# Value rows loaded once into three sets of slots, their block means made from the slots, and a byte copy that joins the first expert's weights

## The chip, the cores and the metric

The kernel runs on one core of a Trainium2 chip. The metric is the device time of one execution in microseconds (us): 640.8 us, the median of three runs (639.45 to 641.47).

## What is computed

Three stages follow each other. Sparse attention on two batches, 8 heads, 768 positions and 64 values a head: a query sees the keys less than 16 positions away and, for each of the 24 blocks of 32 positions, the maximum of the block's keys; the values are the local ones and the block means of v. Then a first expert with the Mish activation, then a second one with a product of two projections.

```
k_sum = k.reshape(B, H, nb, 32, D).max(axis=3)
v_sum = v.reshape(B, H, nb, 32, D).mean(axis=3)
mask_l = abs(pos[:, None] - pos[None, :]) < 16
scores_s = scale * einsum('bhsd,bhnd->bhsn', q, k_sum) + log(32)
a = softmax(concatenate([where(mask_l, scale * q k^T, -1e9), scores_s]))
x = a @ concatenate([v, v_sum])            # 1536 tokens x 512
h = x @ w_in; x = (h * tanh(softplus(h))) @ w_out     # d_ff 2048
out = ((x @ w_a) * (x @ w_b)) @ w_out2                # d_ff 1536
```

The weights of the experts arrive as 64-bit floats and every product of an expert is made of three matmuls of rounded 32-bit parts (high by high, low by high, high by low).

## The kernel before

**Attention** goes through six groups of 256 queries, three for each batch (g0 to g2, g3 to g5), and in each group through four pairs of heads, which gives 24 small batches, numbered here from 0. For each of them TensorE makes the scores (`batch_s`, lines 509 and 513, 16 matmuls), VectorE adds the mask (line 524), ScalarE takes four exponentials (line 531), VectorE divides (lines 534 to 538), TensorE transposes (`batch_o`, line 553, 4 instructions), ScalarE or VectorE copies the result out of PSUM, and TensorE multiplies by the values (line 566, 8 matmuls). A matmul of plain 32-bit floats is two instructions in the trace (x8 is four of them). The result is split into a rounded high part and a rest (lines 578 and 579), the input of the first expert.

**The values** lie in two sets of slots (`vw_o`), 120 partitions high: 96 window rows of v for each of four units of 64 queries, and 24 rows for the block means. `load_windows` loads the windows (576 to 768 KB a group, the first and last unit of a batch by a DMA of 160 KB of its own). The means come from a second reading of v: `prep_v` loads a batch of v in three pieces of 512 KB into borrowed slots and multiplies them by a pooling matrix (line 443, 24 matmuls a batch), `keep_v` copies the result from PSUM, and `spread_v` copies it into both sets of slots by four DMAs of 48 KB each on SyncE's queue, 8 in a batch.

**The first expert's weights** are cut into 16 slices of `w_in` and 16 of `w_out`. `load_w` loads a slice (512 KB) into one of three staging slots, joins the two 32-bit words of each number (ScalarE at line 604, VectorE at lines 606, 609 and 612), and writes the rounded high part (line 618) and the rest (line 620) into a slot of 1024 columns. Slices 0 to 4 are used by three blocks of tokens in turn (256, 256 and 512 tokens), between and beside the batches of attention.

**The order** is written by a planner, `Plan`: each operation has a key (a due time), costs and dependencies, and `emit` hands each engine its instructions in the order that the planner's model gives. On the chip every engine, and SyncE's queue of DMAs, goes through its list in that order and waits at the head. Until the planner's time 21 it puts in dummy matmuls (`fill`, line 397) where TensorE would be free.

The diff touches `Plan.emit` (line 206), the slots (lines 269, 310, 316), `dma`, `consts`, `prep_v`, `keep_v`, `spread_v`, `load_windows`, `batch_o`, `load_w` and the due times from line 687.

Of the kernel before, what the change touches and what calls it, by code (L numbers as in the profile page):

```python
# [14 lines left out]
I32 = mybir.dt.int32  # L15
AF = mybir.ActivationFunctionType
# [18 lines left out]
class Plan:  # L35
# [49 lines left out]
    def emit(self):  # L85
# [32 lines left out]
        while done < n:  # L118
# [84 lines left out]
            if delay:  # L203
                dma_free = max(dma_free, end + self.DMA_LEAD) + delay
                end = dma_free + self.DMA_TAIL
                landed.append(end)
# [18 lines left out]
def attention_mish_moe_bilinear_moe(  # L225
# [23 lines left out]
    U = 64  # L249
# [19 lines left out]
    TOT, N_BASE, N_EXT = 53184, 16, 10  # L269
# [40 lines left out]
    vw_o = [take(GU * HD) for _ in range(2)]  # L310
# [5 lines left out]
    NPO = 2 * NB - P // BLK  # L316
# [14 lines left out]
    def dma(key, dst, src, r=(), w=(), nbytes=0):  # L331
        pl.add(key, [("SP", 0.48, lambda env: nc.sync.dma_start(out=dst, in_=src))],  # L332
               r=r, w=w, delay=nbytes / 3.3e5)
# [24 lines left out]
    def consts(env):  # L358

        nc.gpsimd.memset(mask, 0.0)  # L360
        nc.gpsimd.memset(mask[:, :, WK:SW], math.log(BLK) / SCALE)
        for h in range(2):
            m = mask[h * U:(h + 1) * U, :, 0:WK]
            nc.gpsimd.affine_select(
                out=m, in_=m, pattern=[[0, 3], [1, WK]], base=-1,
                channel_multiplier=-1, compare_op=ALU.is_ge, fill=NEG)
            nc.gpsimd.affine_select(
                out=m, in_=m, pattern=[[0, 3], [-1, WK]], base=2 * WIN - 1,
                channel_multiplier=1, compare_op=ALU.is_ge, fill=NEG)
# [10 lines left out]
        mid = pool[:, C0:C0 + P // BLK]  # L380
        nc.gpsimd.memset(mid, 1.0 / BLK)
        nc.gpsimd.affine_select(out=mid, in_=mid, pattern=[[-BLK, P // BLK]], base=0,
                                channel_multiplier=1, compare_op=ALU.is_ge, fill=0.0)
        nc.gpsimd.affine_select(out=mid, in_=mid, pattern=[[BLK, P // BLK]], base=BLK - 1,
                                channel_multiplier=-1, compare_op=ALU.is_ge, fill=0.0)
# [43 lines left out]
    def prep_v(key, kd, b, pieces):  # L429


        name = ("vs", b)
        t0 = 0
        for o, n in pieces:
            src = v[b, t0 * P:(t0 + n) * P, :].rearrange("(t p) c -> p t c", p=P)
            dma(kd + 0.01 * t0, ar(o, n, HD), src, w=[sb(o, n * HD)], nbytes=n * P * HD * 4)
            for i in range(n):
                t = t0 + i

                def mm(env, t=t, o=o, i=i):  # L440
                    c = C0 - P // BLK * t
                    for p in range(NP):
                        nc.tensor.matmul(bank[env[name]][32 * p:32 * p + NB, 0:P], pool[:, c:c + NB],  # L443
                                         ar(o + i * HD + p * P, P), start=(t == 0), stop=(t == S // P - 1),
                                         skip_group_check=True)

                pe(key, 0.3, mm, r=[sb(pool_o, NPO), sb(o, n * HD)], w=[name],
                   alloc=(name,) if t == 0 else ())
            t0 += n
        assert t0 == S // P  # L450

    def keep_v(key, b):
        name = ("vs", b)
        copy(key, P, lambda env: ar(vm_o, P), lambda env: bank[env[name]][:, 0:P], w=[name, sb(vm_o, P)], free=[name])

    def spread_v(key, s):

        for p in range(NP):
            src = ar(vm_o, P)[32 * p:32 * p + NB, :].unsqueeze(1).to_broadcast([NB, GU, P])
            dma(key + 0.01 * p, ar(vw_o[s], GU, HD)[WK:SW, :, p * P:(p + 1) * P], src,  # L460
                r=[sb(vm_o, P)], w=[("vsum", s, p)], nbytes=NB * GU * P * 4)

    def load_windows(key, g):

        b, gi = divmod(g, NG)
        s = g % 2
# [76 lines left out]
    def batch_o(key, g, p):  # L543
# [15 lines left out]
        vs = g % 2  # L559
# [27 lines left out]
    def load_w(first, kind, c):  # L587
# [9 lines left out]
        if BITS64:  # L597
# [6 lines left out]
            act(key, 512, lambda env: nc.scalar.activation(out=hw, in_=hw, func=AF.Copy, scale=2.0 ** -112),  # L604
                r=[sb(so, 1024)], w=[("hw", so)])
            dve(key, 512, lambda env: nc.vector.tensor_scalar(
                out=f.bitcast(U32), in0=f.bitcast(U32), scalar1=29, scalar2=None,
                op0=ALU.logical_shift_right), fast=True, r=[sb(so, 1024)], w=[("f", so)])
            dve(key, 512, lambda env: nc.vector.scalar_tensor_tensor(  # L609
                out=f.bitcast(U32), in0=hw.bitcast(U32), scalar=3, in1=f.bitcast(U32),  # L610
                op0=ALU.logical_shift_left, op1=ALU.bitwise_or), r=[("hw", so), sb(so, 1024)], w=[("f", so)])
            dve(key, 512, lambda env: nc.vector.scalar_tensor_tensor(  # L612
                out=f.bitcast(U32), in0=hw.bitcast(U32), scalar=0x80000000, in1=f.bitcast(U32),
                op0=ALU.bitwise_and, op1=ALU.bitwise_or), r=[("hw", so), sb(so, 1024)], w=[("f", so)])
        else:
            f = ar(so, 512)
            dma(key - 3.0, f, w_dram[kind][c], w=[sb(so, 512), ("f", so)], nbytes=P * 2048)
        copy(key, 512, lambda env: r32(ar(o + 512, 512)), lambda env: f, fast=True, only='ACT',
             r=[("f", so), sb(so, 1024)] + ext, w=[sb(o + 512, 512)])
        dve(key, 512, lambda env: nc.vector.tensor_sub(out=r32(ar(o, 512)), in0=f, in1=ar(o + 512, 512)),  # L620
            r=[sb(o + 512, 512), ("f", so), sb(so, 1024)], w=[sb(o, 512)])
# [66 lines left out]
    for b in range(B):  # L688
        g0 = NG * b
        if b == 0:  # L690
            pieces = [(T_S[0], 2), (T_S[2], 2), (T_L[1], 2)]
            kv, kd, ev = 8.0, 6.0, 1.5
        else:
            pieces = [(T_S[0], 2), (Y1, 2), (T_S[0], 2)]
            kv, kd = bt[g0, 0] - 8.0, bt[g0, 0] - 16.0
            ev = end_o(g0 - 2)
        at_time(ev, lambda kv=kv, kd=kd, b=b, x=pieces: prep_v(kv, kd, b, x))
        at_time(ev, lambda kv=kv, b=b: keep_v(kv + 0.5, b))
        for i in range(2):
            ev = end_o(g0 - 2 + i) if b else 1.6  # L700
            at_time(ev, lambda k=max(kv, ev), x=(g0 + i) % 2: spread_v(k + 1.0, x))
# [5 lines left out]
    for g in range(B * NG):  # L707
        kq, kw = (0.6, 4.0) if g == 0 else (bt[g, 0] - 10.0, bt[g, 0] - 4.0)
        at_time(end_s(g - 2) if g >= 2 else 1.0, lambda k=kq, g=g: load_q(k, g))
        at_time(end_o(g - 2) if g >= 2 else 1.5, lambda k=kw, g=g: load_windows(k, g))  # L710
# [246 lines left out]
```

## Time and profile before

| | us |
|---|---|
| median of three runs | 640.8 |
| the profiled execution | 640.17 |
| its span, first to last instruction | 638.1 |
| TensorE busy | 624.9 |
| VectorE busy | 319.1 |
| ScalarE busy | 264.0 |
| GpSimd busy | 6.5 |

The span is 2.07 us shorter than the execution's own time. TensorE is busy for 98% of it; the page's slices show the other engines and the DMA engines busy in the first quarter and mostly free later. Matmuls of dummies count as busy too, so the first slices are to be read by line.

### The profile page before, as it was taken

What the parts mean: (1) busy time and instruction counts of PE and PEld (TensorE: products, weight loads), DVE (VectorE), ACT (ScalarE), POOL (GpSimd) and SP (SyncE); (2) the same over time, 40 slices, a digit from 0 to 9 for tenths busy, and PEclk for the clock granted to TensorE, in tenths of its full rate; (3) what the DMA queues carried; (4) which work ended last, traced back from release to release, by engine and by line L of the source; (5) the groups of instructions that cost most, each with busy time, mean ns of one, the idle gap of its engine ahead of it and who ended that gap; (6) DMA issues with size and microseconds to landing.
All of it is one profiled execution on the core that took longest, in us unless ns stands there. A gap on an engine that the chain in (4) does not pass through costs nothing.

```text
span 638.1 us, 9894 instructions
## 1 busy us (share of the span) xinstructions
PE 624.9 (98%) x3966; PEld 514.1 (81%) x3969; DVE 319.1 (50%) x749; ACT 264.0 (41%) x577; POOL 6.5 (1%) x30
## 2 busy tenths in 40 slices
PE   8879999999999999999999999999999999999997
PEld 4568988888888888888888888888888888888886
DVE  6778989889892121148898511215651111112212
ACT  4579998776562322245565212113431112111110
POOL 2000000000000000000000000000000000000000
PEclk9979999999999999999999999999999999999999
DMA  8799442255460000004563200001400000100101
GB/s 296 204 323 293 130 123 68 74 173 193 156 198 0 1 0 2 1 33 149 181 196 102 67 0 2 1 0 67 138 28 0 1 0 24 43 1 1 66 1 66
DMA packets 21661, 54.24 MB, mean 85 GB/s; under 512 B 1968, under 2 KB 6576, under 8 KB 21616
## 3 DMA queue, kind: packets, MB, share of 16 engines
q1 hardware_dynamic: 21616, 53.62, 26.3%
q8 instruction: 31, 0.51, 0.3%
q14 instruction: 14, 0.11, 0.1%
HBM read 49.68 MB, written 3.15 MB: 83 GB/s over the span
## 4 chain that ended last, share of the span: by engine, by line
PE 93%; DMA 5%; DVE 1%; SPq 0%; issue 0%; ACT 0%
PE bank L759 51%; PE bank L806 21%; PE bank L871 15%; DMA attn<-in_qT_dram 2%; PE bank L566 2%; PE bank L553 2%; PE bank L509 1%; DMA arena<-in_w_in_dram 1%; DMA arena<-in_kT_dram 1%; PE bank L513 0%; SPq L332 0%; PE bank L443 0%; DVE attn L346 0%; DVE arena L892 0%; DVE arena L609 0%
## 5 line engine op out<-in xcount | busy, mean ns | idle before, releaser
L759 PE MATMUL bank<-rounded 128*128 128x512 f32 (+1 forms) x1068 | 240.7, 379 | 0.0
L759 PEld LDWEIGHTS bank<-rounded 128*128 128x128 f32 x1068 | 193.6, 190 | 37.6 <-ACT arena L788 0.3
L345 ACT CAST rounded<-arena 128x512 fp32r<-128x512 f32 (+1 forms) x129 | 79.1, 622 | 191.3 <-PE bank L871 124.1
L759 PE MATMUL bank<-rounded,wext 128*128 128x512 f32 x432 | 102.8, 389 | 0.0
L806 PE MATMUL bank<-rounded 128*128 128x512 f32 (+1 forms) x456 | 99.4, 365 | 0.0
L759 PEld LDWEIGHTS bank<-rounded,wext 128*128 128x128 f32 x432 | 81.1, 188 | 16.8
L855 DVE TENSOR_TENSOR arena<-arena,bank 128x512 f32<-128x512 f32 x36 | 24.8, 688 | 130.0 <-PE bank L759 129.9
L806 PEld LDWEIGHTS bank<-rounded 128*128 128x128 f32 x456 | 78.2, 188 | 13.8 <-issue 0.2
L791 DVE TENSOR_TENSOR rounded<-arena,rounded 128x512 fp32r<-128x512 f32 (+1 forms) x53 | 33.8, 638 | 73.8 <-ACT rounded L345 73.8
L871 PE MATMUL bank<-rounded 128*128 128x512 f32 x288 | 69.0, 389 | 0.0
L871 PEld LDWEIGHTS bank<-rounded 128*128 128x128 f32 x288 | 54.1, 188 | 11.2
L858 DVE TENSOR_TENSOR rounded<-arena,rounded 128x512 fp32r<-128x512 f32 x36 | 24.9, 691 | 62.4 <-ACT rounded L345 57.4
L788 ACT ACTIVATE arena<-bank 128x512 f32<-128x512 f32 (+1 forms) x53 | 29.5, 563 | 58.2 <-PE bank L759 58.1
L604 ACT ACTIVATE arena<-arena 128x512 f32<-128x512 f32 x68 | 46.5, 686 | 15.7 <-DMA arena<-in_w_out_dram 6.7
L854 ACT COPY arena<-bank 128x512 f32<-128x512 f32 x36 | 21.2, 589 | 73.3 <-PE bank L759 73.2
L609 DVE SCALAR_TENSOR_TENSOR arena<-arena 128x512 uint32<-128x512 uint32 x68 | 46.8, 688 | 6.5 <-ACT arena L604 4.8
L612 DVE SCALAR_TENSOR_TENSOR arena<-arena 128x512 uint32<-128x512 uint32 x68 | 46.8, 688 | 0.9
L806 PE MATMUL bank<-rounded,wext 128*128 128x512 f32 x180 | 43.2, 389 | 0.0
L806 PEld LDWEIGHTS bank<-rounded,wext 128*128 128x128 f32 x180 | 33.8, 188 | 7.0
L531 ACT ACTIVATE attn<-attn 128x120 f32<-128x120 f32 x96 | 36.6, 385 | 5.6 <-DVE attn L524 5.6
L620 DVE TENSOR_TENSOR rounded<-arena,rounded 128x512 fp32r<-128x512 f32 x47 | 32.1, 685 | 10.1 <-ACT rounded L345 9.8
L871 PE MATMUL bank<-wext,rounded 128*128 128x512 f32 x144 | 34.3, 389 | 0.0
(61 smaller groups left out, 394.1 us busy)
## 6 DMA issues: line engine op xcount, KB each, us to landing
arena<-in_w_out_dram SPq DMA_DIRECT2D x28, 512.0 KB
arena<-in_w_in_dram SPq DMA_DIRECT2D x16, 512.0 KB
arena<-in_w_a_dram SPq DMA_DIRECT2D x12, 512.0 KB
arena<-in_w_b_dram SPq DMA_DIRECT2D x12, 512.0 KB
arena<-in_kT_dram SPq DMA_DIRECT2D x8, 384.0 KB
arena<-in_v_dram SPq DMA_DIRECT2D x6, 512.0 KB
out_dram<-arena SPq DMA_DIRECT2D x12, 256.0 KB
attn<-in_qT_dram SPq DMA_DIRECT2D x5, 512.0 KB
```

Source lines behind the costliest of these rows:

```text
L345: alts = [("ACT", act_us(n), lambda env: nc.scalar.copy(out=dst(env), in_=src(env))), ("DVE", dve2_us(n) if fast else dve_us(n), lambda en ...
L531: act(key, SW + 90, lambda env, x=x: nc.scalar.activation(out=s[:, x, :], in_=s[:, x, :], func=AF.Exp, scale=-1.0, bias=negm[:, x:x + 1], ...
L604: act(key, 512, lambda env: nc.scalar.activation(out=hw, in_=hw, func=AF.Copy, scale=2.0 ** -112), r=[sb(so, 1024)], w=[("hw", so)])
L609: dve(key, 512, lambda env: nc.vector.scalar_tensor_tensor(out=f.bitcast(U32), in0=hw.bitcast(U32), scalar=3, in1=f.bitcast(U32), op0=ALU. ...
L612: dve(key, 512, lambda env: nc.vector.scalar_tensor_tensor(out=f.bitcast(U32), in0=hw.bitcast(U32), scalar=0x80000000, in1=f.bitcast(U32), ...
L620: dve(key, 512, lambda env: nc.vector.tensor_sub(out=r32(ar(o, 512)), in0=f, in1=ar(o + 512, 512)), r=[sb(o + 512, 512), ("f", so), sb(so, ...
L759: nc.tensor.matmul(like(dst, b), lt, rt, start=(j == 0), stop=(j == 3 * KC - 1))
L788: act(ka, n, lambda env: nc.scalar.activation(out=g, in_=hp(env), func=AF.Mish), w=[hn, sb(lo, n)], free=[hn], table="mish")
L791: dve(ka, n, lambda env: nc.vector.tensor_sub(out=r32(gl), in0=g, in1=gh), r=[sb(lo, n), sb(ho, n)], w=[sb(go, n)])
L806: nc.tensor.matmul(yp, lt, r32(rt), start=(fst and j == 0), stop=(lst and j == 2))
L858: dve(ka, n, lambda env: nc.vector.tensor_sub(out=r32(gl), in0=pp, in1=gh), r=[sb(po, n), sb(ho, n)], w=[sb(ho + 512, n)])
L871: nc.tensor.matmul(bank[env[on]], lt, rt, start=(first and j == 0), stop=(last and j == 2))
```

## The change

v is no longer read a second time. There are three sets of slots, one for each group of a batch, so all windows of a batch lie in SBUF at once, and the means are made from the window rows that the slots hold (`means`, 16 matmuls a group, 48 a batch). The first group of the first batch gets its means by four copies on ScalarE and VectorE; the other 20 copies are DMAs on GpSimd's queue. For the first expert's weights ScalarE copies one byte of the low word into the high word, and VectorE joins the words with two operations in place of three; the scaled value goes to a slot of its own (`T_S`), and the staging slot comes free one step earlier. The weight slots are 14 from the start and 12 after attention, in place of 16 and 10.

```diff
-            if delay: ... landed.append(end)
+                if e == "SP":
+                    landed.append(end)
-    TOT, N_BASE, N_EXT = 53184, 16, 10
+    TOT, N_BASE, N_EXT = 53184, 14, 12
-    vw_o = [take(GU * HD) for _ in range(2)]
+    vw_o = [take(GU * HD) for _ in range(NG)]
-    def prep_v(key, kd, b, pieces): ...   # three loads of v, 24 matmuls
-    def keep_v(key, b): ...
+    def means(key, g):
+        b, gi = divmod(g, NG)
+        name, vs = ("vs", b), g % NG
+        def mm(env):
+            for u in range(GU):
+                c, vw = C0 - U // BLK * (GU * gi + u), ar(vw_o[vs], GU, HD)
+                for p in range(NP):
+                    nc.tensor.matmul(bank[env[name]][32 * p:32 * p + NB, 0:P], pool[0:WK, c:c + NB],
+                                     vw[0:WK, u, p * P:(p + 1) * P], start=(gi == 0 and u == 0),
+                                     stop=(gi == NG - 1 and u == GU - 1), skip_group_check=True)
+        pe(key, 0.25 * GU, mm, r=[sb(pool_o, NPO)] + [("vw", vs, j) for j in range(3)], w=[name],
+           alloc=(name,) if gi == 0 else ())
+        if gi == NG - 1:
+            copy(key, P, lambda env: ar(vm_o, P), ...)
-            dma(key + 0.01 * p, ar(vw_o[s], GU, HD)[WK:SW, :, p * P:(p + 1) * P], src, ...)
+            if engines:
+                copy(key, GU * P, lambda env, d=dst: d, lambda env, x=src: x, r=[sb(vm_o, P)], w=[("vsum", s, p)])
+            else:
+                dma(key + 0.01 * p, dst, src, eng="POOL", ...)
+            if kind in ("in", "out"):
+                _, fo = nxt("wf", T_S)
+                f = ar(fo, 512)
+                word, byte = hw.bitcast(I32), ar(so, 1024).bitcast(U8).rearrange("p (n b) -> p n b", b=8)
+                act(key, 512, lambda env: nc.scalar.activation(out=f, in_=hw, func=AF.Copy, scale=2.0 ** -112), ...)
+                act(key, 512, lambda env: nc.scalar.copy(out=byte[:, :, 4], in_=byte[:, :, 3]), ...)
+                dve(key, 512, lambda env: nc.vector.tensor_scalar(
+                    out=word, in0=word, scalar1=5, scalar2=-0x7ffffff9,
+                    op0=ALU.arith_shift_right, op1=ALU.bitwise_and), fast=True, ...)
+                dve(key, 512, lambda env: nc.vector.scalar_tensor_tensor(
+                    out=f.bitcast(I32), in0=f.bitcast(I32), scalar=3, in1=word,
+                    op0=ALU.logical_shift_left, op1=ALU.bitwise_or), ...)
-            bt[g, p] = vis_t[0] + 1.5 * p
+            bt[g, p] = vis_t[0] - 3.0 + 1.0 * p
-        at_time(end_o(g - 2) if g >= 2 else 1.5, lambda k=kw, g=g: load_windows(k, g))
+            at_time(ev, lambda k=kw, g=g: load_windows(k, g))
+            at_time(max(ev, end_o(g0 - 1)) if b else 1.6, lambda k=kw + 5.0, g=g: means(k, g))
```

SyncE's queue, before, from the first window load to the queries of g1 and beyond: `in_v_dram` into `arena` is v for the means, into `attn` the windows, and `attn<-attn` the spreading of the means.

```order
L332 DMA arena<-in_v_dram 128x2x512 x2
L332 DMA attn<-in_v_dram 80x512
L332 DMA attn<-in_v_dram 96x3x512
L332 DMA arena<-in_w_out_dram 128x1024
L332 DMA arena<-in_w_in_dram 128x1024
L332 DMA attn<-in_qT_dram 128x4x256
L332 DMA attn<-attn 24x4x128 x8
L332 DMA arena<-in_w_out_dram 128x1024
```

The same place of the same queue after the change (the `in_qT_dram` row is again the queries of g1).

```order
L335 DMA attn<-in_v_dram 96x4x512
L335 DMA attn<-in_v_dram 80x512
L335 DMA attn<-in_v_dram 96x3x512
L335 DMA arena<-in_w_out_dram 128x1024
L335 DMA attn<-in_v_dram 80x512
L335 DMA attn<-in_qT_dram 128x4x256
L335 DMA arena<-in_w_in_dram 128x1024
L335 DMA arena<-in_w_out_dram 128x1024
```

The two pieces of v and the eight spreads are gone from the queue, the windows of g1 and g2 have moved ahead of the queries of g1, and the second slice of `w_in` stands behind these queries, no longer ahead of them.

ScalarE's list after the change, from the copy of the means out of PSUM (`attn<-bank_64 128x128`): L608 is the scaling of a weight slice, L610 the byte copy, L530 the exponentials, and the casts from a bank split the results of attention.

```order
L348 COPY attn<-bank_64 128x128
L348 COPY attn<-attn 24x4x128 x2
L348 CAST rounded<-arena 128x512
L608 ACTIVATE arena<-arena 128x512
L348 CAST rounded<-bank_61 128x256
L348 CAST rounded<-bank_62 128x256
L610 COPY arena<-arena 128x512
L348 COPY attn<-bank_63 120x512
L348 COPY attn<-bank_64 120x512
L530 ACTIVATE attn<-attn 128x120 x2
```

The list before, from the same kind of place: the cast of the first `w_in` slice, then two scalings of slices, and the first split of a result.

```order
L345 CAST rounded<-arena 128x512
L604 ACTIVATE arena<-arena 128x512 x2
L345 CAST rounded<-arena 128x512
L345 CAST rounded<-bank_67 128x256
L345 CAST rounded<-arena 128x512
L345 CAST rounded<-bank_61 128x256
L345 COPY attn<-bank_62 120x512
L345 COPY attn<-bank_63 120x512
```

A byte copy stands in the list behind each scaling, two copies spread the means, and the scaling of the second `w_in` slice now stands directly ahead of the splits of g0 and of the copies of its last two transposes.

## Rows read from the trace of the kernel before

**Rows 1.** The page: busy time by engine, and the chain by engine.

```profile
PE 624.9 (98%) x3966; PEld 514.1 (81%) x3969; DVE 319.1 (50%) x749; ACT 264.0 (41%) x577; POOL 6.5 (1%) x30
...
PE 93%; DMA 5%; DVE 1%; SPq 0%; issue 0%; ACT 0%
```

**Rows 2.** Windows: stretch, length; busy PE, PEld, DVE, ACT, POOL; PE clock, DMA share, GB/s.

```profile
23.80:26.40 2.60, 0.02 (x1) 0.00 (x0) 2.07 (x5) 1.02 (x2) 0.00 (x0) 1.00 0.38 80
35.40:39.00 3.60, 0.69 (x18) 0.39 (x17) 2.28 (x5) 2.22 (x10) 0.00 (x0) 1.00 1.05 379
39.00:46.00 7.00, 6.22 (x68) 5.42 (x72) 6.69 (x18) 5.37 (x15) 0.00 (x0) 0.51 1.06 283
46.00:634.00 588.00, 587.99 (x3423) 490.25 (x3420) 284.47 (x624) 237.45 (x487) 1.04 (x2) 1.00 0.21 69
```

**Rows 3.** Timeline of TensorE and ScalarE: the waits for DMAs.

```profile
26.49 0.40 PE L509 MATMUL bank<-arena,attn 64*64 64x96 f32 x8 [2.67 <-DMA attn<-in_qT_dram]
...
36.78 0.69 ACT L604 ACTIVATE arena<-arena 128x512 f32<-128x512 f32 x1 [1.44 <-DMA arena<-in_w_in_dram]
...
38.09 0.64 PE L443 MATMUL bank<-arena,attn 128*24 128x128 f32 x16 [2.66 <-DMA arena<-in_v_dram]
```

**Rows 4.** Timeline of SyncE's queue: start, length, line, DMA, count.

```profile
10.95 0.38 SPq L332 DMA_DIRECT2D attn<-in_qT_dram  x1
19.14 8.11 SPq L332 DMA_DIRECT2D attn<-attn  x8
27.35 0.47 SPq L332 DMA_DIRECT2D arena<-in_w_out_dram  x1
```

**Rows 5.** Timeline of TensorE: attention, then the expert's first product and the means.

```profile
27.18 1.15 PE L566 MATMUL bank<-attn 120*64 120x64 f32 x32
28.26 1.09 PE L553 MATMUL bank<-attn 128*120 128x128 f32 x8
29.28 0.40 PE L509 MATMUL bank<-arena,attn 64*64 64x96 f32 x8
...
59.01 1.70 PE L759 MATMUL bank<-rounded 128*128 128x256 f32 x12
60.64 0.42 PE L443 MATMUL bank<-arena,attn 128*24 128x128 f32 x8
60.99 4.58 PE L759 MATMUL bank<-rounded 128*128 128x256 f32 x36
65.41 1.03 PE L553 MATMUL bank<-attn 128*120 128x128 f32 x8
```

**Rows 6.** Stretches in which v (first) and window rows (second) are mostly loaded.

```profile
8.00:13.00 5.00, 4.80 (x93) 2.93 (x94) 4.50 (x25) 2.80 (x16) 0.00 (x0) 1.00 1.04 407
14.00:19.00 5.00, 4.84 (x78) 2.36 (x78) 3.40 (x15) 4.22 (x17) 0.00 (x0) 1.00 1.06 232
```

**Rows 7.** Timeline of ScalarE: one instruction of each kind and the start of the next.

```profile
41.25 1.28 ACT L788 ACT_TABLE_LOAD   x1
42.54 0.38 ACT L788 ACTIVATE arena<-bank 128x256 f32<-128x256 f32 x1
42.82 0.37 ACT L345 CAST rounded<-bank 128x256 fp32r<-128x256 f32 x1
...
56.88 0.67 ACT L604 ACTIVATE arena<-arena 128x512 f32<-128x512 f32 x1
57.44 0.65 ACT L345 CAST rounded<-arena 128x512 fp32r<-128x512 f32 x1
57.99 0.40 ACT L531 ACTIVATE attn<-attn 128x120 f32<-128x120 f32 x1
...
58.38 0.38 ACT L531 ACTIVATE attn<-attn 128x120 f32<-128x120 f32 x1
```

**Rows 8.** Groups by line and form: VectorE's joining of a slice.

```profile
L609 DVE SCALAR_TENSOR_TENSOR arena<-arena 128x512 uint32<-128x512 uint32 x68 | 46.8, 688 | 6.5 <-ACT arena L604 4.8
...
L606 DVE TENSOR_SCALAR arena<-arena 128x512 uint32<-128x512 uint32 x68 | 28.7, 422 | 6.0 <-DMA arena<-in_w_out_dram 2.9 <-DMA arena<-in_w_in_dram 1.9 <-DMA arena<-in_w_b_dram 1.0
```

More of the change, by code (lines that the diff above doesn't have):

```diff
@@ L329, in attention_mish_moe_bilinear_moe, with dma @@
     pl = Plan()
-    def dma(key, dst, src, r=(), w=(), nbytes=0):
-        pl.add(key, [("SP", 0.48, lambda env: nc.sync.dma_start(out=dst, in_=src))],
+    def dma(key, dst, src, r=(), w=(), nbytes=0, eng="SP"):
+        q, cost = (nc.sync, 0.48) if eng == "SP" else (nc.gpsimd, 1.0)
+        pl.add(key, [(eng, cost, lambda env: q.dma_start(out=dst, in_=src))],
                r=r, w=w, delay=nbytes / 3.3e5)
@@ L379, in consts @@
         nc.gpsimd.memset(pool, 0.0)
-        mid = pool[:, C0:C0 + P // BLK]
+        mid = pool[:, C0:C0 + U // BLK]
         nc.gpsimd.memset(mid, 1.0 / BLK)
-        nc.gpsimd.affine_select(out=mid, in_=mid, pattern=[[-BLK, P // BLK]], base=0,
+        nc.gpsimd.affine_select(out=mid, in_=mid, pattern=[[-BLK, U // BLK]], base=-WIN,
                                 channel_multiplier=1, compare_op=ALU.is_ge, fill=0.0)
-        nc.gpsimd.affine_select(out=mid, in_=mid, pattern=[[BLK, P // BLK]], base=BLK - 1,
+        nc.gpsimd.affine_select(out=mid, in_=mid, pattern=[[BLK, U // BLK]], base=WIN + BLK - 1,
                                 channel_multiplier=-1, compare_op=ALU.is_ge, fill=0.0)
@@ L427, in prep_k @@
             op=ALU.max, axis=AX.X), r=[sb(o, SK)], w=[sb(ksum_o[p], NB)])
[L429 to L456, printed above, removed]
+    def means(key, g):
[11 more added lines that the diff above has]
+        if gi == NG - 1:
+            copy(key, P, lambda env: ar(vm_o, P), lambda env: bank[env[name]][:, 0:P], w=[name, sb(vm_o, P)],
+                 free=[name])
@@ L458, in spread_v @@
+    def spread_v(key, s, engines=False):
         for p in range(NP):
             src = ar(vm_o, P)[32 * p:32 * p + NB, :].unsqueeze(1).to_broadcast([NB, GU, P])
[L460 to L461 removed]
+            dst = ar(vw_o[s], GU, HD)[WK:SW, :, p * P:(p + 1) * P]
+            if engines:
+                copy(key, GU * P, lambda env, d=dst: d, lambda env, x=src: x, r=[sb(vm_o, P)], w=[("vsum", s, p)])
+            else:
+                dma(key + 0.01 * p, dst, src, eng="POOL",
+                    r=[sb(vm_o, P)], w=[("vsum", s, p)], nbytes=NB * GU * P * 4)
@@ L601, in load_w @@
             f, hw = raw[:, :, 0], raw[:, :, 1]
[L604 to L611, printed above, removed]
@@ L689, in attention_mish_moe_bilinear_moe @@
         g0 = NG * b
[L690 to L701, printed above, removed]
+        for i in range(NG):
+            g = g0 + i
+            kw = 3.0 + 1.5 * i if b == 0 else bt[g0, 0] - 14.0 + 3.0 * i
+            ev = end_o(g - NG) if b else 1.5
+            at_time(ev, lambda k=kw, g=g: load_windows(k, g))
+            at_time(max(ev, end_o(g0 - 1)) if b else 1.6, lambda k=kw + 5.0, g=g: means(k, g))
+        for i in range(NG):
+            at_time(end_o(g0 - 1) + eps if b else 1.7,
+                    lambda k=(12.0 if b == 0 else bt[g0, 0] - 2.0) + 3.0 * i, b=b, i=i: spread_v(k, i, b == 0 and i == 0))
         for p in range(NP):
```

38 lines of the change are left out of this document (28 added, 10 removed).

## Prediction

> **What bounds the kernel now.** First the page: TensorE is busy for 98% of the span and holds 93% of the chain that ended last [rows 1]. Then the windows, to see where the other 2% and the dummies lie [rows 2]. From 46 us to 634 us TensorE is busy for 587.99 of 588.00 us: nothing there can be gained by a faster transfer or a freer engine, only by less matmul work. Ahead of that it stands idle twice, 2.6 us up to 26.4 and some 2.9 of the 3.6 us from 35.4, and from 39 to 46 its clock is granted at 0.51, the 1.2 GHz level. So the time is set by two things: how much matmul work there is, and at which moment of the first 60 us TensorE has done a given part of it. The timelines name what it waits for: at 26.49 the queries of g1, at 38.09 v for the means of the second batch, while ScalarE waits for a weight slice up to 36.78 [rows 3]. SyncE's queue shows why: between the issue of these queries at 10.95 and the next slice at 27.35 stand the eight spreads, which wait for the means and then take 8.11 us, about 1.0 us each [rows 4].
>
> The unit of comparison is a place that both orders reach with the same work done: the end of the fifth product of the first block (line 759, five times 12 matmuls). Before it is at 60.64 [rows 5]; the last four matmuls of the second batch's means follow it. By then the scores of batches 0 to 11, the outputs of 0 to 7 and three second products are done. After the change the same are done there, only the means differ: 44 of 48 matmuls before, 64 of 96 after.
>
> **The change part by part.**
>
> *More matmuls.* The means take 96 matmuls in place of 48. Four of them (x8) take from 60.64 to 60.99, so 0.0875 us each [rows 5]. The first batch's 24 more stand among dummies and cost nothing there unless they end after the queries land. The second batch's 24 more stand in the busy stretch: +2.1 us, nothing hides them. At the place of comparison the change has 32 matmuls of means ahead (2.8 us), before has 4 (0.35): it must be there 2.45 us earlier, at 58.2, to be equal.
>
> *Transfers.* v's six loads of 512 KB go. But look at what must be in before the expert can run on: before, all that is issued up to the queries of g1 has landed when the wait ends at 26.49 [rows 3]. After, the same set up to the second `w_in` slice differs only in that 1536 KB of v is swapped for 1504 KB of windows of g1 and g2, which have moved ahead. v came at 407 GB/s, 3.9 us; windows came at 232 GB/s, 6.6 us [rows 6]. So that slice lands between 26.5 (if windows can run as v did) and 29.2; I take 28.5, near the windows' row, less 0.7 because the eight spreads (0.39 MB) leave this queue. The queries of g1 land one slice (0.52 MB, 1.3 us) ahead of it, at 27.2, and the last window of g2 at about 25.8. The last 16 matmuls of means end at 27.2. The stall of 26.49 therefore doesn't go; it ends 0.7 us later.
>
> *The spreads off SyncE's queue.* What goes is the blocked queue after 10.95. What is late next is not a load: the third `w_in` slice, for which ScalarE waited until 36.78 [rows 3], now stands two loads behind the second one and lands 3 to 4 us earlier, and ScalarE comes to it later still.
>
> *The spread for g0 on the engines.* Four copies of 512 columns, two on ScalarE and two on VectorE, 0.55 us each from start to start [rows 7], after a copy out of PSUM: ready at 28.7, against 28.4 for the end of two batches of scores. They cost 0.3 us.
>
> *The byte copy.* For each of 32 slices VectorE loses one operation of 688 ns and keeps one of 688 and one of 422 [rows 8]; ScalarE gains one of 512 columns. Neither a byte copy nor the two-step form of the 422 ns operation is in the trace. The copy is bounded by a quarter of a slot (0.14, four times fewer bytes) and by 0.69; I take 0.55, the slot of its neighbours. The other is bounded by 422 and 688; I take 422. The sum over both engines hardly moves, but in the first 50 us ScalarE is the one that now has the longer list.
>
> *ScalarE's list from 28.6.* It stands at the scaling of the second `w_in` slice until that lands. Up to the last exponential of batch 7 there follow, in the order shown, 9 operations of 512 columns at 0.55, four casts of 256 at 0.27, 16 exponentials at 0.39 (57.99 to 58.38): 5.0 + 1.1 + 6.2 = 12.3, with 0.4 of waits for the outputs of g0: 41.3. Then eight of 512 columns, two of 256, the table load of 1.28, one Mish and one cast of 256 (0.3 each): 4.4 + 0.5 + 1.3 + 0.6 = 6.8, so 48.1, and VectorE's rest of it 48.6.
>
> *TensorE after that.* Second product of slice 0 at 1.47 us (a third of 60.99 to 65.41), fourth first product, two batches of scores at 0.6, two second products, fifth first product: 5 x 1.47 + 1.2 = 8.55 [rows 5]. 48.6 + 8.55 = 57.15, against 58.2: 1.1 us are gained. TensorE's clock is taken as full throughout.
>
> *The second batch.* Its means now need the windows of g5, which can be issued only when the outputs of g2 have left that slot. A load of 736 KB at 232 GB/s takes 3.3 us, and what lies between its issue and its first byte comes on top, which no row isolates; between the two stand scores, part of a second product and one first product, 4.6 us. Bounds are 0 and 2 us; I put 0.5 on it. Behind the means 4.6 us of matmuls stand ahead of the first output of g3; spreads at 1.0 us each, with 1 to 2 us to land, keep pace, so nothing on that. VectorE's shorter list later is off the path, since TensorE waits for nobody there. The two slots fewer at the start and two more later leave the sum as it is.
>
> The sum: -1.1 + 0.5 = -0.6 us. The profiled execution took 640.17 (its span of 638.1 and 2.07 around it); after: 639.5. The median shown is 640.8, 0.6 above the profiled execution; against it 639.5 is -0.2%, and I state 639.4.
>
> **The rivals.**
>
> *Windows are slow only in that place.* For it: a rate of 232 in a stretch where v's last piece and a slice are also in flight need not be the windows' own. Against it: the stretch is five us long. Then the second slice lands at 26.5 to 27, ScalarE's list starts 1.7 to 2 us earlier, and all of it is on the path: 637 to 636.5, and with a byte copy nearer its lower bound (five of them between 28.6 and 48.1, up to 0.4 us less each) 635.
>
> *The clock falls.* Slower. Before, TensorE did 0.69 us of work in 3.6 us and was at 1.2 GHz for the 7 us from 39 on, while 2.6 us of idle time up to 26.4 did not bring it down [rows 2]. After the change it has from 36.3 to 44.3, between the second first product and the transposes of batch 7, only some 4.8 us of work in 8, waiting for ScalarE. If the same 7 us at half speed follow, half of the work in them is lost, up to 3.5 us, while I counted them as full: 642 to 643. It decides from any fall longer than 4 us.
>
> *GpSimd's spreads are slow.* Slower. Nothing in the trace shows a DMA issued by GpSimd. SyncE's issues of the same copy bound it from one side (8.11 / 8 = 1.0 us [rows 4]); nothing bounds it from the other. With the second batch the first output of g3 tolerates 2 us for each; at 3 us its four outputs are held up by 0.4, 1.8, 3 and 4 us, the last counts: 643.5. At the first batch 8 of them have over 10 us and don't matter.
>
> VectorE has one operation that runs faster than the others for the same 512 columns, 422 against 688 ns, and it fills 28.7 of VectorE's 319.1 busy us [rows 1, 8]; what it does to another engine beside it, the rows don't show. The Trainium skill has a rule for it (SBUF — State Buffer, "SBUF: two separate sides" and "A bandwidth-pool intuition that's wrong"): GpSimd can't write the descriptors of its DMAs while VectorE holds the port that both share in its faster mode, and such a DMA took some 3.1 us in place of 0.62. By that rule an estimate would come out near this rival's time; by SyncE's row the forecast stands, and no run here shows it yet.
>
> *It doesn't do what it says.* The moved loads and ScalarE's longer list eat all: 640.2 to 641, inside the forecast's range.
>
> **How the numbers follow.** The forecast (637.8 to 641.5) has a chance of 0.45, fast windows 0.27, the clock 0.16, the spreads 0.12. A difference of 0.3% (1.9 us, 638.9 to 642.7 from the median) is about what a measurement of this kernel can tell from no change. Of the forecast's chance a third lies below 638.9; of the fast windows all; of the two slow cases most lies above 642.7. Faster 0.42, same 0.34, slower 0.24. The range goes from 635.0 to 643.5.
>
> **What would show it.** Right: scores of batch 4 at 27 to 28, ScalarE without a gap from 29 to 48, Mish first at 47 to 48, the fifth product ending at 56.5 to 58, clock at 1.00 after 36. Wrong: a second `w_in` slice before 27 (the windows' rate), a stretch at 0.5 (the clock), line 565 waiting for GpSimd's DMAs at some 75 us (the spreads), or a byte copy over 0.7 us.

## The result: 1.2% slower

The changed kernel takes 647.4 us (median of four runs, 647.3 to 649.6), the kernel before 640.3 beside it: a ratio of 1.0118, 95% interval 1.009 to 1.0146. The forecast was 639.4, its range ended at 643.5. The profiled execution took 647.54, with a span of 645.8: 7.7 us longer than before. One execution of e17 below (1041 us at a granted clock of 0.56) is left out of every ratio.

From the page of the changed kernel, the busy times and the chain that ended last; it answers to [rows 1].

```profile
PE 626.3 (97%) x4053; PEld 517.2 (80%) x4057; DVE 307.1 (48%) x727; ACT 294.4 (46%) x603; POOL 17.8 (3%) x50
...
PE 85%; ACT 9%; DMA 4%; issue 1%; SPq 0%; DVE 0%; ACTq 0%
```

ScalarE is busy for 30 us more, and the chain, 93% TensorE before, is now 85% TensorE and 9% ScalarE. The prices by line (busy us, mean ns of one | idle before) say why:

```profile
L610 ACT COPY arena<-arena 128x512 uint8<-128x512 uint8 x32 | 44.1, 1385 | 0.2
...
L615 DVE SCALAR_TENSOR_TENSOR arena<-arena 128x512 int32<-128x512 int32 x32 | 21.9, 686 | 0.3
...
L612 DVE TENSOR_SCALAR arena<-arena 128x512 int32<-128x512 int32 x32 | 13.5, 427 | 21.4 <-ACT arena L610 21.4
```

The byte copy (L610) takes 1.385 us, where I had put 0.55 and a bound of 0.69. The rest of the new join is as [rows 8] had it: 686 ns for the joining operation, 427 for the two-step one that I took at 422. But ahead of the latter VectorE waits 21.4 us in all for L610.

The windows of the changed kernel (busy us of PE, PEld, DVE, ACT, POOL, each with its count; then granted clock, DMA share, GB/s), with the last as in [rows 2]:

```profile
26.50:35.00 8.50, 6.99 (x208) 6.48 (x209) 6.86 (x35) 7.18 (x18) 4.96 (x9) 1.00 0.95 256
35.00:46.00 11.00, 7.28 (x142) 5.86 (x140) 9.39 (x36) 11.00 (x35) 0.00 (x0) 0.99 0.89 270
46.00:60.00 14.00, 12.73 (x157) 11.58 (x158) 10.10 (x28) 12.36 (x23) 0.00 (x0) 0.65 0.49 144
60.00:140.00 80.00, 78.94 (x1065) 68.22 (x1065) 68.47 (x252) 78.20 (x213) 7.43 (x13) 1.00 0.39 117
46.00:634.00 588.00, 585.66 (x3399) 489.00 (x3400) 273.42 (x599) 262.38 (x511) 7.43 (x13) 0.99 0.20 65
```

From 35 to 46 ScalarE is busy for 11.00 of 11.00 us. TensorE, which had no gap from 46 to 634 before, now has 2.3 us of them, and its clock is at 0.65 from 46 to 60 (at 1.2 GHz up to 55.9). The same window of the kernel before, for the one stretch in which it lost time:

```profile
35.00:46.00 11.00, 7.31 (x88) 6.03 (x90) 8.97 (x22) 7.94 (x26) 0.00 (x0) 0.69 1.05 318
```

At 26.5 both kernels stand ahead of the same scores. Count as lost what is idle or not granted (width less busy time times clock). After: 1.5, 3.8, 5.7 and 1.1, together 12.1 us. Before: 6.0 here, nothing in the others. That is 6.1 us more; 24 more matmuls of means in the busy stretch, at 1.07 us for 16 (43.10 below), are another 1.6. The sum of 7.7 is the difference of the spans.

What TensorE waited for from 20 to 200 us (total, times, longest), against [rows 3]:

```profile
PE bank L565 <- ACT attn L348: 2.0, 2, 1.7
PE bank L508 <- DMA attn<-in_qT_dram: 1.6, 1, 1.6
PE bank L552 <- DVE attn L537: 1.3, 1, 1.3
PE bank L565 <- issue: 1.1, 1, 1.1
PE bank L441 <- DVE arena L615: 1.1, 1, 1.1
```

The places on TensorE that the prediction named, beside [rows 5]:

```profile
26.91 0.40 PE L508 MATMUL bank<-arena,attn 64*64 64x96 f32 x8 [1.57 <-DMA attn<-in_qT_dram]
...
33.64 0.39 PE L565 MATMUL bank<-attn 120*64 120x64 f32 x6 [1.10 <-issue]
...
43.10 1.07 PE L441 MATMUL bank<-attn 96*24 96x128 f32 x32 [1.05 <-DVE arena L615]
...
46.50 1.12 PE L565 MATMUL bank<-attn 120*64 120x64 f32 x16 [1.74 <-ACT attn L348]
...
50.49 2.93 PE L773 MATMUL bank<-rounded 128*128 128x256 f32 x12 [0.77 <-ACT arena L802]
...
62.35 1.60 PE L773 MATMUL bank<-rounded 128*128 128x256 f32 x12
```

The stall on the queries of g1 (27.2 forecast) ends at 26.91. The fifth first product, which had to end at 58.2 to be equal and was forecast for 57.15, starts at 62.35 and ends at 63.95. Before it, at 46.50, TensorE has waited for a copy on ScalarE. ScalarE's list just there:

```profile
44.16 0.62 ACT L348 CAST rounded<-arena 128x512 fp32r<-128x512 f32 x1
44.67 1.35 ACT L610 COPY arena<-arena 128x512 uint8<-128x512 uint8 x1
45.74 0.71 ACT L348 COPY attn<-bank 120x512 f32<-120x512 f32 x1
46.32 0.69 ACT L608 ACTIVATE arena<-arena 128x512 f32<-128x512 f32 x1
46.88 0.38 ACT L348 CAST rounded<-bank 128x256 fp32r<-128x256 f32 x1
47.14 1.40 ACT L610 COPY arena<-arena 128x512 uint8<-128x512 uint8 x1
48.22 0.52 ACT L348 CAST rounded<-bank 128x256 fp32r<-128x256 f32 x1
48.76 1.28 ACT L802 ACT_TABLE_LOAD   x1
```

Each row follows the one before without a gap. The copy at 45.74 that TensorE waits for stands behind a byte copy, the table load of Mish behind another: it comes at 48.76, where the forecast's list had it at 46.2 (41.3 + 4.4 + 0.5). Five byte copies stand in that list, as counted, each 0.83 us dearer than priced: 4.2 us. The table load is 2.6 us late and not 4.2, because the list starts 0.4 us earlier than forecast (28.20) and its other terms are some 1.2 us shorter.

### The profile page after: what moved, and what is told of

It is laid out like the page before. It is cut to its first block, busy times and chain, and to the rows that moved or that the text cites. A ratio compares the mean times of both kernels' runs of the same rounds, so it can differ in the third digit from the quotient of the medians.

```text
span 645.8 us, 10086 instructions
## 1 busy us (share of the span) xinstructions
PE 626.3 (97%) x4053; PEld 517.2 (80%) x4057; DVE 307.1 (48%) x727; ACT 294.4 (46%) x603; POOL 17.8 (3%) x50
## 4 chain that ended last, share of the span: by engine, by line
PE 85%; ACT 9%; DMA 4%; issue 1%; SPq 0%; DVE 0%; ACTq 0%
PE bank L773 48%; PE bank L820 19%; PE bank L885 15%; ACT attn L530 3%; DMA attn<-in_qT_dram 2%; ACT arena L610 2%; ACT rounded L348 1%; DMA attn<-in_v_dram 1%; PE bank L565 1%; ACT arena L608 1%; PE bank L508 1%; PE bank L552 1%; ACT L802 1%; ACT attn L348 0%; ACT arena L802 0%
## 5 line engine op out<-in xcount | busy, mean ns | idle before, releaser
L773 PE MATMUL bank<-rounded 128*128 128x512 f32 (+1 forms) x996 | 225.2, 379 | 0.9 <-ACT arena L802 0.8
L773 PEld LDWEIGHTS bank<-rounded 128*128 128x128 f32 x996 | 180.3, 190 | 35.7 <-ACT arena L802 1.0
L348 ACT CAST rounded<-arena 128x512 fp32r<-128x512 f32 (+1 forms) x122 | 75.3, 624 | 184.1 <-PE bank L885 123.0
L773 PE MATMUL bank<-rounded,wext 128*128 128x512 f32 x504 | 120.1, 389 | 0.0
L773 PEld LDWEIGHTS bank<-rounded,wext 128*128 128x128 f32 x504 | 94.6, 188 | 19.6
L820 PE MATMUL bank<-rounded 128*128 128x512 f32 (+1 forms) x420 | 91.2, 365 | 0.0
L820 PEld LDWEIGHTS bank<-rounded 128*128 128x128 f32 x420 | 71.8, 191 | 12.3 <-DVE attn L523 0.2
L820 PE MATMUL bank<-rounded,wext 128*128 128x512 f32 x216 | 51.9, 389 | 0.0
L885 PE MATMUL bank<-rounded 128*128 128x512 f32 x216 | 51.9, 389 | 0.0
L885 PE MATMUL bank<-wext,rounded 128*128 128x512 f32 x216 | 51.1, 389 | 0.0
L820 PEld LDWEIGHTS bank<-rounded,wext 128*128 128x128 f32 x216 | 40.6, 188 | 8.4
L885 PEld LDWEIGHTS bank<-rounded 128*128 128x128 f32 x216 | 40.6, 188 | 8.4
L885 PEld LDWEIGHTS bank<-wext,rounded 128*128 128x128 f32 x216 | 40.6, 188 | 8.4
L610 ACT COPY arena<-arena 128x512 uint8<-128x512 uint8 x32 | 44.1, 1385 | 0.2
L530 ACT ACTIVATE attn<-attn 128x120 f32<-128x120 f32 x96 | 36.7, 386 | 5.1 <-DVE attn L523 5.0
L620 ACT ACTIVATE arena<-arena 128x512 f32<-128x512 f32 x36 | 24.7, 687 | 13.0 <-DMA arena<-in_w_out_dram 5.4
```

Of the source, the lines that this page charges most:

```text
L348: alts = [("ACT", act_us(n), lambda env: nc.scalar.copy(out=dst(env), in_=src(env))), ("DVE", dve2_us(n) if fast else dve_us(n), lambda en ...
L530: act(key, SW + 90, lambda env, x=x: nc.scalar.activation(out=s[:, x, :], in_=s[:, x, :], func=AF.Exp, scale=-1.0, bias=negm[:, x:x + 1], ...
L610: act(key, 512, lambda env: nc.scalar.copy(out=byte[:, :, 4], in_=byte[:, :, 3]), r=[sb(so, 1024), sb(fo, 512)], w=[("hw", so)])
L773: nc.tensor.matmul(like(dst, b), lt, rt, start=(j == 0), stop=(j == 3 * KC - 1))
L820: nc.tensor.matmul(yp, lt, r32(rt), start=(fst and j == 0), stop=(lst and j == 2))
L885: nc.tensor.matmul(bank[env[on]], lt, rt, start=(first and j == 0), stop=(last and j == 2))
```

## The experiments

All ratios are to the kernel before, timed beside each (median 639.5 to 640.9), with 95% intervals.

**The price, in the same order.** Two kernels shorten the byte copy and leave every engine's order as it is.

```diff
-  nc.scalar.copy(out=byte[:, :, 4], in_=byte[:, :, 3])
+  nc.scalar.copy(out=byte[:, 0:128, 4], in_=byte[:, 0:128, 3])   # e1; 0:256 in e15
```

Expected of e1:

> The changed kernel in the same order of instructions, but each byte copy moves only 128 of the 512 columns (the low word of the other columns is joined without that byte, so that part of the weights' last bits is left out). Theory A (the byte copy's price): it takes 1.385 us where 0.55 was counted, 32 times on ScalarE, which is full from 35 to 100 us; the rest of the loss (waits of TensorE at 43, 46, 50, 72 us, the half clock from 46 on) follows from it. With a quarter of the columns I expect 0.45 to 0.6 us a copy and a time of 638.5 to 641.5. Theory B (the transfers and the moved loads, with 48 more matmuls): the price hardly matters, 645 to 648. In between, the share of each is read off.

Expected of e15:

> The changed kernel in the same order with 256 of the 512 columns in each byte copy (the joined low bits of the other columns are left out). The copy should take 0.79 us (0.189 + 256 x 2.336 ns). If the price acts in proportion, 642.1 + (0.79 - 0.49) / (1.385 - 0.49) x 5.3 = 643.9; if only from the point where ScalarE is full, 641.5 to 642.5; 643 to 644.7 for the first.

```profile
L610 ACT COPY arena<-arena 128x128 uint8<-128x128 uint8 x32 | 15.3, 488 | 0.2
```

This row (e1) and the whole copy's 1385 ns give 0.189 us + 2.34 ns a column; e15's mean of 783 ns lies near that line (788). e1 took 642.08 (1.0021, 1.0004 to 1.0039), e15 644.01 (1.0051, 1.0028 to 1.0073), near the 643.9 of the proportion; its interval (642.1 to 644.9) just reaches the other expectation. From 0.488 to 1.385 us the price is worth 5.3 us by the medians, and no point is seen from which it starts to count. e5 and e6 below are such a pair too, with the spreads on SyncE's queue: 640.78 and 645.02, so 4.2 us. Theory A holds for about three quarters of the loss (5.3 of 7.1 us). The rest of it is there with the short copy: e1 is still no faster than the kernel before.

**One part alone.** e2 joins all weights the old way (`if False:` for `if kind in ("in", "out"):`); e3 puts the new join, with its slot, into the kernel before.

Expected of e2:

> The change of v, its slots and its spreads alone; all weights are joined as before, by three operations on VectorE. Theory A: no byte copies, so 639 to 642, with 2 us of it for the 24 matmuls in the busy stretch and at most 1 us of stall at the first batch. Theory B: as the changed kernel, 645 to 648.

Expected of e3:

> The byte copy alone, v loaded, averaged and spread as in the kernel before (the eight warming matmuls go to eight banks in place of one). Theory A: most of the loss is here, 644 to 648, with ScalarE busy for over 9.8 of 10 us from 40 to 120 us. Theory B: 639 to 641.5.

e3 took 647.79 (1.0116, 1.0096 to 1.0135): the byte copy alone loses as much as the whole change. e2 took 643.28 (1.0049, 1.0027 to 1.0072), a little more than Theory A allowed: v's part loses too. The two overlap (0.49% and 1.16% against 1.18% together), as losses can that are both waits ahead of the same matmuls; no run isolates that. Here, and wherever an operation moves to another engine, the planner writes a new order too.

**The byte copy elsewhere.** e4: `nc.gpsimd.tensor_copy` in place of `nc.scalar.copy`; e7: `nc.vector.tensor_copy`.

Expected of e4:

> The changed kernel with the byte copies on GpSimd, which is otherwise nearly idle; nothing in the traces shows its price there. Theory A: ScalarE loses 44 us of work; if the copy takes under 3 us on GpSimd, 637 to 641. Theory B: 645 to 648. A third outcome: the copy takes over 4 us there or slows VectorE beside it, and the join waits for it: above 646 with VectorE waiting for GpSimd.

Expected of e7:

> The changed kernel with the byte copies on VectorE. The traces show no byte operation there. If it is as slow as on the other two engines (1.39 and 1.46 us), VectorE's list grows by 0.7 us a slice over the kernel before and TensorE waits for VectorE: 646 to 651. If it takes 0.4 to 0.7 us, ScalarE is relieved and VectorE has no more than before: 638 to 643.

e4, by line:

```profile
L610 POOL COPY arena<-arena 128x512 uint8<-128x512 uint8 x32 | 45.6, 1456 | 96.6 <-ACT arena L608 94.2 <-DVE arena L615 2.3
...
L615 DVE SCALAR_TENSOR_TENSOR arena<-arena 128x512 int32<-128x512 int32 x32 | 26.4, 824 | 0.4
...
L612 DVE TENSOR_SCALAR arena<-arena 128x512 int32<-128x512 int32 x32 | 19.9, 622 | 9.4 <-POOL arena L610 9.4
```

On GpSimd it takes 1.456 us, and VectorE's operations beside it grow from 686 to 824 and from 427 to 622 ns: 651.24 (1.0169, 1.0143 to 1.0195), the third outcome. The Trainium skill (SBUF — State Buffer, "Who interferes with whom") says that VectorE's operations in its two-port modes, or with two inputs in SBUF, share a pair of ports with GpSimd, and that whichever comes second waits. These two rows agree in that both grow; the wait itself isn't visible in them. On VectorE (e7) it takes 754 ns, just over what I had allowed for the good case, and the time is 646.28 (1.0090, 1.0058 to 1.0122), above the range for that case.

**What makes it dear.** e8 times seven forms of copy of 128x512.

> The changed kernel with two weight slots fewer and seven forms of copy of 128x512, each twice on ScalarE and on VectorE, on memory of their own after 400 us; only their durations are read. What makes the byte copy slow? Stride alone: then 16-bit and 32-bit copies with the same 8-byte step take 1.2 us or more (the scaling of a slice with that step takes 0.70, which speaks against it). Writing single bytes apart: then only the forms that write bytes with a step are slow, reading them into 32-bit words takes some 0.6. Bytes as a type: then the copy of 512 bytes in a row is as slow, 1.2 to 1.4.

By line (L938 ScalarE, L941 VectorE; the uint8 rows mix a step of eight bytes and bytes in a row). They ran from 137 us on, one execution only:

```profile
L938 ACT COPY arena<-arena 128x512 uint16<-128x512 uint16 x2 | 3.2, 1587 | 0.0
L938 ACT CAST arena<-arena 128x512 uint8<-128x512 f32 x2 | 3.1, 1530 | 0.0
L938 ACT COPY arena<-arena 128x512 f32<-128x512 f32 x4 | 2.9, 736 | 1.3 <-DVE arena L941 1.3
...
L941 DVE COPY arena<-arena 128x512 uint16<-128x512 uint16 x2 | 1.5, 762 | 0.0
L941 DVE CAST arena<-arena 128x512 uint8<-128x512 f32 x2 | 1.5, 755 | 0.0
L938 ACT CAST arena<-arena 128x512 f32<-128x512 uint8 x2 | 1.4, 706 | 0.0
...
L941 DVE CAST arena<-arena 128x512 f32<-128x512 uint8 x2 | 0.8, 422 | 0.0
```

The single uint8 copies on ScalarE, the first with the step, the second in a row:

```profile
137.14 1.51 ACT L938 COPY arena<-arena 128x512 uint8<-128x512 uint8 x1
...
153.26 0.70 ACT L938 COPY arena<-arena 128x512 uint8<-128x512 uint8 x1
```

Reading bytes with a step into 32-bit words costs what any copy does (706 and 422 ns), and so do bytes in a row (0.70). Writing bytes or 16-bit words apart costs about twice that: 1.5 to 1.6 us on ScalarE, 0.76 on VectorE, even from a 32-bit source (1530, 755). So neither the step nor the type alone makes it dear, but the two together in what is written. The second expectation is right.

**The planner told the price.** e11 gives the byte copy 1.4 us in the planner.

```diff
-  act(key, 512, lambda env: nc.scalar.copy(...), ...)
+  pl.add(key, [("ACT", 1.4, lambda env: nc.scalar.copy(...))], ...)
```

> The changed kernel, with whole byte copies, and the planner told that one takes 1.4 us (0.6 before), so that the order of all engines is planned with it. If the loss comes from an order planned with a wrong price: 641 to 643. If it comes from ScalarE's list being too long whatever the order, from 35 to 100 us: 645 to 648.

645.54 (1.0091, 1.0068 to 1.0115), inside the second range. The wrong price in the planner isn't the main cause: the order planned with the right one loses about as much.

**The spreads' queue.** In e1 TensorE stands still in a place where nothing in the profile holds it. Its timeline:

```profile
24.39 0.40 PE L508 MATMUL bank<-arena,attn 64*64 64x96 f32 x8
...
29.44 1.03 PE L565 MATMUL bank<-attn 120*64 120x64 f32 x26
34.10 0.59 PE L565 MATMUL bank<-attn 120*64 120x64 f32 x6 [3.62 <-issue]
34.62 5.48 PE L773 MATMUL bank<-rounded 128*128 128x256 f32 x24
```

Scores of batch 4 start 2.1 us ahead of the kernel before, and then that lead is lost: 13 of 16 matmuls of L565 run, three wait 3.62 us for "issue", and the first two products behind them run at the half clock (5.48 us, 3.13 in the kernel before). The changed kernel has the same gap at the same matmul (33.64 above, 1.10 us). The instruction queue's part of the DMA rows of e1, from 31 to 33 us (packets, MB, share):

```profile
q8 instruction: 1, 0.02, 5.2%
```

That is one packet of 16 KB, from 31.09 to 32.75 in the trace. That such packets are TensorE's code is inferred from their count: in the kernel before 15 of them go with 1899 matmul instructions and 1898 weight loads from 200 to 630 us, where VectorE and ScalarE together have 448. e5 and e6 put all spreads on SyncE's queue (`eng="POOL"` left out), e5 with e1's short copy and the same order on TensorE, VectorE and ScalarE.

Expected of e5:

> As the run with 128 of 512 columns in each byte copy (the joined low bits of the other columns are left out), but all twenty spreads by DMA stand on SyncE's queue; TensorE, VectorE and ScalarE have the same order. Theory C (code): in that run TensorE stood still for 3.62 us from 30.47, in the middle of a row of matmuls that wait for nothing, until 1.35 us after a 16 KB packet of the instruction queue that ran beside the GpSimd spreads, and was then at half the clock for 5 us. If the GpSimd queue delays that code, the stall and the half clock go: 637 to 640. Theory D (any small packets do it): the stall stays, 641 to 643. Theory E (the blocked queue): the spreads hold up the next slices on SyncE's queue as before the change, 642 to 646.

Expected of e6:

> The changed kernel with all byte copies whole and the twenty spreads on SyncE's queue. Theory C: the 1.10 us stall at 32.5 goes, but ScalarE bounds what follows: 645.5 to 647.5, a gain of 0 to 2 us. Theory E: 648 or more. If it falls to 642 the byte copy's price is not the main cause.

e5's timeline:

```profile
31.13 1.15 PE L565 MATMUL bank<-attn 120*64 120x64 f32 x32
32.21 1.81 PE L773 MATMUL bank<-rounded 128*128 128x256 f32 x13
...
42.84 0.91 PE L441 MATMUL bank<-attn 96*24 96x128 f32 x24 [2.08 <-DMA attn<-in_v_dram]
```

The wait in L565 is gone and the first product follows at 32.21. The same packet runs earlier: from 28.55 to 29.82 in e5 and 28.40 to 30.03 in e6, against 31.09 to 32.75 in e1 and 30.56 to 32.12 in the changed kernel; in e6 the wait is gone too. What is left is a wait for the windows of g3, 2.08 us at 42.84; I had put 0.5 on those of g5 and nothing on these. The time is 640.78 (1.0012, 0.9994 to 1.003), in e6 645.02 (1.0096, 1.0061 to 1.0131). The traces, one execution each, agree with Theory C; the times don't separate e5 from e1, nor e6 from the changed kernel, so how much of the time the late code costs stays open. It isn't GpSimd's queue alone: in e7 TensorE waited 1.97 us for a packet of code (56.03 to 57.33) with no spread near and the DMA engines busy for all of that stretch (share 1.04 from 54 to 58). The Trainium skill (Runtime: NRT & Kernel Launch, "Instruction fetch mechanics") calls the cost of crossing from one such block of code to the next mostly hidden. From 200 to 630 us of the kernel before it is (TensorE busy for all 430 us), and in these places it was not.

**Versions without GpSimd's queue.** e9: v alone with spreads on SyncE; e10: the same with windows counted 1.42 times longer by the planner (`nbytes=1.42 * ...`); e12: e7 with spreads on SyncE.

Expected of e9:

> The change of v alone (weights joined as before, by VectorE), with all spreads by DMA on SyncE's queue. Theory C (a late packet of code beside GpSimd's spreads): no wait inside a row of TensorE at 30 to 34; but in the run of v alone that wait was not there either, so the time stays near that run's 643.3: 640.5 to 643. If the spreads on GpSimd's queue cost more than that wait (late landings), 638 to 640.

Expected of e10:

> As the run before it, but the planner counts the windows of v 1.42 times longer (232 GB/s in place of 330), which moves the second batch's first means behind other work. Theory: TensorE's wait for windows at 40 to 43 (2.0 us in three of the runs) is what is left of the loss; without it 638 to 640.5, about the kernel before. If the wait only moves to ScalarE's or VectorE's lists, which are full there, 641 to 643.

Expected of e12:

> The byte copies on VectorE (754 ns there) and the spreads on SyncE's queue. In the run with the copies on VectorE and the spreads on GpSimd TensorE waited 3.1 us for a Mish of ScalarE and 2.0 us for code. Theory: the code wait goes and the rest stays, 642 to 645; VectorE's list is then 0.07 us a slice longer than before the change, ScalarE's no longer. Rival: both waits come from the order, and it goes to 640 to 641.

646.49 (1.0104, 1.008 to 1.0128), 646.05 (1.0096, 1.0074 to 1.0117) and 645.88 (1.0095, 1.0072 to 1.0117): e9 and e10 are misses. All three write new orders, and each waits elsewhere (e9 3.2 us for windows, and from 20 to 100 us ScalarE 7.5 for weight slices; e10 1.1 for windows, 5.7 for VectorE; e12 4.5 for windows). v alone is slower in each order tried, but by 0.5 to 1%, and why one order is worse isn't settled.

**Which part of v.** e16 does each of the 48 matmuls of the kernel before twice, with half the weight; e13 moves only its spreads to GpSimd's queue, e14 makes the first set's by engines as well. (In e3, e13, e14 and e16 to e18 the eight warming matmuls go to eight banks. In e13, e14, e17 and e18 the planner, which prices GpSimd's issues in another way, also writes a new order.)

```diff
-            dma(key + 0.01 * p, ..., src, r=..., w=...)
+            dma(key + 0.01 * p, ..., src, eng="POOL", r=..., w=...)      # e13, e17, e18
-                    for p in range(NP):
+                    for j in range(2):                                   # e16
+                        for p in range(NP):
```

Expected of e13:

> The kernel before, with only the queue of its sixteen spreads changed from SyncE to GpSimd (the warming matmuls go to eight banks). If the blocked queue of SyncE is what the first 60 us pay for, the queries of g1 and the third slice come earlier: 636.5 to 639. If the later landing of GpSimd's spreads (4 to 7 us from issue in the changed kernel) holds up the first outputs: 641 to 645. If neither: 639.5 to 641.5.

Expected of e14:

> As the run before it, but the first set of slots gets its means by four copies on ScalarE and VectorE. If the spreads' landing is what counts, this gives 636.5 to 639; if the two lists are what counts, 1 to 2 us more than the run before it.

Expected of e16:

> The kernel before with each of the 48 matmuls of the means done twice (with half the weight), 24 of the added ones in the busy stretch. At 0.0875 us each, as I priced them, +2.1: 642.2 to 643; at the 0.063 us that the changed kernel shows, +1.5: 641.5 to 642.3; hidden under the waits for v and the queries: 640 to 641.

e16: 641.91 (1.0028, 1.0008 to 1.0048), so 1.6 us, the size that the timeline of the changed kernel gives; the interval (0.5 to 3.1 us) doesn't rule out the 2.1 of the forecast. e13: 638.19 (0.9971, 0.9949 to 0.9993): the queue, with the order that goes with it, gains. e14: 639.08 (0.9986, 0.9967 to 1.0005), not told apart from e13.

e17 is e13 again; e18 prices GpSimd's issue at 0.6.

Expected of e17:

> The kernel before with its spreads on GpSimd's queue, a second time. If the gain is real, 0.995 to 0.999 of the kernel before; if the first was chance, 0.999 to 1.002.

Expected of e18:

> The same, with the planner told that an issue on GpSimd takes 0.6 us (0.58 measured) in place of 1.0, which moves many instructions. If the queue is what gains, whatever the order, again 0.995 to 0.999; if it was the order, it can go either way, 0.998 to 1.006.

e17: 637.53 (0.9951, 0.9935 to 0.9967); e18: 638.96 (0.9975, 0.9953 to 0.9997). So the gain came again, and with a second order too. No run has such an order without the queue, or the eight banks alone, so neither is ruled out as part of it. e17's kernel is faster than the kernel before and the changed one. SyncE's queue in e17, against [rows 4], and its windows:

```profile
11.07 0.38 SPq L334 DMA_DIRECT2D attn<-in_qT_dram  x1
...
22.97 0.33 SPq L334 DMA_DIRECT2D arena<-in_w_out_dram  x1
...
26.98 0.33 SPq L334 DMA_DIRECT2D arena<-in_w_in_dram  x1
```

```profile
26.50:35.00 8.50, 6.68 (x186) 5.58 (x187) 6.97 (x35) 5.63 (x22) 0.44 (x1) 1.00 1.05 299
35.00:46.00 11.00, 9.42 (x155) 7.76 (x155) 9.98 (x33) 9.63 (x31) 0.08 (x1) 1.00 1.06 273
46.00:60.00 14.00, 14.00 (x195) 12.58 (x195) 13.14 (x56) 12.44 (x39) 2.97 (x5) 1.00 0.96 302
60.00:140.00 80.00, 80.00 (x1000) 69.33 (x999) 73.85 (x245) 65.88 (x187) 2.85 (x5) 1.00 0.36 114
```

The slices that stood behind 8.11 us of spreads are issued from 22.97 on, not 27.35, and SyncE's queue no longer holds eight spreads. TensorE loses 1.8, 1.6 and nothing, 3.4 us against 6.0, and its clock stays full. The 1.8 is a wait for the spreads themselves (2.16 us, up to 28.32), which land 6.0 us after their issue (median). By these rows the gain lies there: the mean granted clock is 0.992 before and 0.998 in e17, worth 3.8 us of 640, and 3.3 were measured.

## Why the prediction was wrong, by its steps

1. *Byte copy:* this is the step that failed: "bounded by a quarter of a slot (0.14, four times fewer bytes) and by 0.69; I take 0.55". It took 1.385, past the 0.7 that the prediction itself named as a sign of being wrong. The upper bound came from 32-bit operations that read with the same step; none of the rows writes single bytes, so it was no bound. Of the 8.0 us between 639.4 and 647.4, 5.3 lie between copies of 0.488 and 1.385 us.
2. *ScalarE's list:* the mechanism and the count were right (five byte copies, Mish behind them); 4.2 us of price, less 1.6 that other terms were too long, put the table load at 48.76 and not 46.2.
3. *TensorE after that:* "clock is taken as full" was wrong as a consequence. Waiting for that list, TensorE did 7.28 us of work in the 11 up to 46 and then was at half the clock, from 45.7 to 55.9. That is 4.5 of its 12.1 lost us (12.73 x 0.35; before it was 2.3).
4. *More matmuls:* right in kind, 0.067 us each and not 0.0875 (1.6 and not 2.1).
5. *Transfers:* right: queries at 26.91 against 27.2, second slice at 28.20 against 28.5.
6. *Second batch:* the 0.5 was put on the wrong windows. In the changed kernel and in e5 nothing waited for those of g5; those of g3, which had no term, held TensorE for 2.1 us in e5. In the changed kernel no such wait shows, since TensorE comes to them later.
7. *Rivals:* windows were not fast (the second slice at 28.20, not before 27). The clock rival was right in kind, TensorE waiting for ScalarE and then at 1.2 GHz, with a fall of 10.2 us where 7 were taken, but behind the dear byte copy. GpSimd's issues are not slow:

```profile
26.16 4.78 POOL L335 DMA_DIRECT2D attn<-attn  x8 [19.68 <-ACT attn L348]
```

0.60 us each, less than SyncE's 1.0. From issue to landing they took 6.4 us (median of 20), not the 1 to 2 that I allowed; TensorE waited for none of them in the changed kernel. By the rule in the Trainium skill (SBUF — State Buffer, "A bandwidth-pool intuition that's wrong") such a DMA beside a copy of VectorE took some 3.1 us in place of 0.62. The issues above don't show it, and what makes the landings long, waiting descriptors or full DMA engines, no run separates. What I had not thought of is that code for TensorE competes with those transfers.

With a byte copy of 0.49 us, less than the 0.55 of the sum, the kernel takes 642.1 (e1), or 640.8 with the spreads on SyncE's queue (e5), so the rest of the sum was off by 1.4 to 2.7 us and the gain would not have come at the forecast price either. The traces show the late code in e1 and the windows of g3 in e5; what each is worth in time stays open.

## What to carry to other kernels

The width of what an operation writes is part of its form: where no row shows an operation that writes bytes or half words apart, leave the upper bound open, and price it by itself before it goes onto a full engine. In a stage where an engine is busy for all of it, what is added to its list shows in the time (here 642.1, 644.0 and 647.4 us for 0.49, 0.78 and 1.39 us a copy), and a lower clock of TensorE adds to that. Of a change with several parts try each alone: here the smallest, the spreads' queue, came with a gain of 0.3 to 0.5%, and the rest of the change hid it.

## What the runs showed of the hardware

- Writes of 8 or 16 bits with a step of 8 bytes: 1.39 to 1.6 us for 512 columns on ScalarE, 0.75 to 0.76 on VectorE, and 1.46 for bytes on GpSimd; bytes in a row take 0.70 on ScalarE. Stepped reads of bytes into 32-bit words cost nothing extra (0.71 and 0.42).
- Packets of 16 KB, by their count TensorE's code, come through the same 16 DMA engines as the data; where these are full one can come late, and TensorE waits (1.1 to 3.6 us; share 0.93 to 1.00 while the packet runs). It need not: in e6 one that ran at a share of 0.96 came in time.
- A GpSimd byte copy slows two of VectorE's operations beside it by 20 and 46% on average (824 against 686, 622 against 427 ns).
